# First key heads loaded in two halves, and a new tie rule, in a ReLU² attention and SwiGLU kernel

## Chip, cores, metric

One core of one Trainium2 chip. Time is device microseconds (us) of one execution. Most runs of one kernel agree within 0.3%. Some are 1 to 6 us longer than the rest of the same kernel; where the records show why, their mean granted TensorE clock is lower (0.98 to 0.996 instead of 0.997 or more). The rule that sorts out slow runs (over 1.5% above the fastest) does not catch all of them, so I call *full-clock* runs those that have a recorded clock of 0.997 or more.

## The reference, cut

```python
scores = matmul(q, k.T) / 8                    # 8 batches x 12 heads, 448 x 64
attn   = maximum(scores, 0) ** 2 / 448
x      = heads of matmul(attn, v), joined       # 3584 tokens x 768
xn     = x / sqrt(mean(x*x) + 1e-6) * rms_g
out    = (silu(xn @ w_gate) * (xn @ w_val)) @ w_out
```

Of the kernel before, what the change touches and what calls it, by code (L numbers as in the profile page):

```python
# [340 lines left out]
def kernel(  # L341
# [35 lines left out]
    JOIN = 300.0  # L377
    LAG = 2800.0
    LAG0 = 2050.0
    FLOOR = 6000.0, 8500.0, 9350.0, 10450.0, 11150.0, 11850.0, 13150.0, 14900.0  # L380
    floors = []
    LASTW = (384, 192, 192)
    A2, A3, A5 = (384, 384), (256, 256, 256), (512, 256)
# [35 lines left out]
    def act_cost(n, per=0.8333):  # L419
        return 172.0 + per * n  # L420

    def dve_cost(n, per=1.0417):
        return 156.0 + per * n
# [22 lines left out]
    def issue(fn, nbytes, run, need=(), rate=None, ahead=8):  # L446

        tok = Tok()
        land = dma["landed"]
        need = list(need) + (land[-ahead:][:1] if len(land) >= ahead else [])  # L450
        land.append(tok)
        rate = rate or (397.0 if run > 512 else 330.0)
        cost = 500.0 + 0.45 * nbytes / run

        def go(e):
            fn()
            end = pl.free["pool"]
            at = max(dma["t"], end + 900.0)
            dma["t"] = at + nbytes / (min(rate, 340.0) if 4600.0 < at < 9000.0 else rate)
            lag = LAG0 if dma["t"] < 5000.0 else 1900.0 if dma["t"] < 6500.0 else LAG  # L460
            at = max(dma["t"] + lag, FLOOR[len(floors)] if len(floors) < len(FLOOR) else 0.0)
            floors.append(at)
            TRACE.append((end - cost, at - end + cost, "dma", "%d" % nbytes))
            return at - end

        pl.task(-1, {"pool": cost}, go, need, tok)
        return tok
# [19 lines left out]
    def landed(nm, b, h0, h1, tok):  # L487
        for h in range(h0, h1):
            ldtok[nm, b].setdefault(h, []).append(tok)
# [26 lines left out]
    def new_k0():  # L516
        if ("k", 0) not in ld:
            ld["k", 0] = fpool.tile([D, H, U * D], BF16, name="k0", tag="k0")
            ldtok["k", 0] = {}
        return ld["k", 0]  # L520

    def load_k0(h0, h1):

        t = new_k0()

        def go():
            nc.gpsimd.dma_start(
                out=t[:, h0:h1], in_=src_of["k"][0, h0:h1].rearrange("h (p u) d -> p h (u d)", p=D)
            )

        landed("k", 0, h0, h1, issue(go, S * (h1 - h0) * D * 4, U * D * 4))
# [84 lines left out]
    def free_bank(bank):  # L616
        def then(end):
            bank.free = end + 60.0
        return then
# [176 lines left out]
    subs = [Sub(0, 0, NA, 0.0), Sub(0, NA, S - NA, 0.0)]  # L796
    subs += [Sub(b, 0, S, 0.0 if b < 2 else PACE) for b in range(1, B)]

    PRIO_R = 3

    def rectify(sub, ps, bank, w, ready, put):

# [12 lines left out]
        def square(e):  # L815
# [6 lines left out]
        a = pl.task(  # L822
            PRIO_R, {"act": act_cost(2 * w), "dve": dve_cost(2 * w)}, relu, [Tok(ready)],
            None, free_bank(bank),
        )
        cost = {"dve": dve_cost(2 * w, 0.52)}
        if sub.b in SQ_ACT:
            cost["act"] = act_cost(2 * w, 0.9)
        pl.task(PRIO_R, cost, square, [a], tok)

# [520 lines left out]
        nc.sync.dma_start(out=g_sb[:], in_=moe_rms_g.rearrange("(kt p) -> p kt", p=P))  # L1351

    copied = {}
    load_k0(0, 4)

    def make_ident(e):
        masks.make_identity(nc, ident[:])
# [178 lines left out]
```

## The kernel before: what the change touches

The kernel lays out a fixed order for every engine when it is built. A small list scheduler in it follows model times: the cost of each operation, and when each load lands (`FLOOR`, a list of assumed landings in order of issue). On the chip each engine then works through its list in that order; a late load holds all that stands behind its first user.

```python
FLOOR = 6000.0, 8500.0, 9350.0, 10450.0, 11150.0, 11850.0, 13150.0, 14900.0   # ns
...
# engine_next: a task that may start first goes first; ties by priority, then by age
key = (s + penalty, prio, seq)
...
# copies of transposed keys and queries have priority 2; relu and square of scores:
PRIO_R = 3
...
def load_k0(h0, h1):                       # keys of batch 0, cast to bf16 on the way
    def go():
        nc.gpsimd.dma_start(out=t[:, h0:h1], in_=...)
    landed("k", 0, h0, h1, issue(go, ...))
...
load_qf(0, 4, nc.sync)                     # float queries, heads 0 to 3
cast(0, 4, [Tok(3600.0)])
cast(4, HQ, [Tok(7400.0)])                 # heads 4 to 7, assumed there at 7.4 us
...
load_k0(0, 4)

def make_ident(e):
    masks.make_identity(nc, ident[:])      # on GpSimd
    mark = nc.gpsimd.nop()                 # lets ScalarE issue the second query load
    tc.add_manual_dep(nc.scalar.nop().ins, mark.ins.name, pl.behind)
    load_qf(4, HQ, nc.scalar)
# then, on GpSimd in this order: k4-8 q8-12 k8-12 v0-4 v4-12 Q, weights, batch 1 ...
```

When TensorE has nothing to do before the FFN starts, it runs *fillers* (psB): matmuls on constants, meant to keep its clock up. Their number at each place is fixed with the order, so keys that land early wait until the fillers ahead of them are done.

## Time and profile before

| | before |
|---|---|
| runs (us) | 494.52, 435.56, 435.29; later 435.11, 434.88, 435.52 |
| span of the profiled run | 433.6 us |
| first transpose of keys on TensorE | 6.29 us |
| keys 4 to 8 first transposed | 8.82 us |
| first product with the values (AV) | 12.38 us |
| first FFN matmul | 23.82 us |

The last row matters most: after it TensorE has no idle time worth naming and the same work whatever the change does, so what is won or lost up to there shows at the end. The run of 494.52 us stands alone and its cause is not known. The profile lines are in the prediction.

### The profile page before, as it was taken

The page shows a single profiled execution, that of the slowest core. Times are in us where ns is not written, and L with a number is a line of the kernel's source. Part 1 is how long each engine was busy: PE and PEld are TensorE (multiplying, and loading weights), DVE is VectorE, ACT ScalarE, POOL GpSimd, SP SyncE. Part 2 cuts the span into 40 slices and gives each one's busy share as a digit, 9 for nine tenths or more (in the row PEclk, how much of TensorE's full clock was granted, in tenths as well). Part 3 has the DMA queues.
Part 4 walks back from the last instruction along what each step waited for, and adds up shares of the span by engine and source line. Part 5 has one row for each costly group of instructions (what it writes and reads, how often), then busy time and mean ns, then how long its engine had stood idle before and what let it go on. Part 6 is the DMA issues. An engine that isn't in the chain of part 4 may idle for free.

```text
span 433.6 us, 12546 instructions
## 1 busy us (share of the span) xinstructions
PE 428.8 (99%) x5570; PEld 315.1 (73%) x5570; DVE 268.2 (62%) x440; ACT 249.7 (58%) x353; POOL 78.2 (18%) x97
## 2 busy tenths in 40 slices
PE   8999999999999999999999999999999999999996
PEld 6688878954589655985578855795569955699996
DVE  3999994488764676747854578567854577442200
ACT  4887774476653675757743676576744567342222
POOL 7543402062160160006200340001000000000000
PEclk9999999999999999999999999999999999999999
DMA  9999999799699599189917991167103200020023
GB/s 148 193 198 195 203 193 126 146 173 113 100 175 193 109 142 61 49 131 110 117 40 171 136 159 10 39 115 109 18 22 91 74 2 2 2 74 2 2 74 109
DMA packets 134805, 44.68 MB, mean 103 GB/s; under 512 B 104096, under 2 KB 131296, under 8 KB 134752
## 3 DMA queue, kind: packets, MB, share of 16 engines
q0 software_dynamic: 94448, 24.16, 57.6%
q1 hardware_dynamic: 39808, 19.50, 22.2%
q8 instruction: 43, 0.70, 0.7%
q10 hardware_dynamic: 496, 0.24, 0.2%
q14 instruction: 10, 0.08, 0.1%
HBM read 48.76 MB, written 11.01 MB: 138 GB/s over the span
## 4 chain that ended last, share of the span: by engine, by line
PE 98%; DMA 1%; issue 0%; ACT 0%; POOLq 0%
PE psO L147 26%; PE psg L147 26%; PE psv L147 25%; PE psAV L976 9%; PE psS L869 7%; PE psT L672 1%; PE psB L1481 1%; DMA k<-in_k_dram 1%; PE psR L890 1%; PE psSS L1158 0%; PE psSS L1082 0%; PE psT L670 0%; ACT ost L1288 0%; POOLq L1520 0%
## 5 line engine op out<-in xcount | busy, mean ns | idle before, releaser
L147 PE MATMUL psg<-xn,wg_sb 64*128 64x448 bf16 (+1 forms) x1296 | 170.9, 329 | 0.0
L147 PE MATMUL psv<-xn,wv_sb 64*128 64x448 bf16 (+1 forms) x1296 | 170.9, 329 | 0.0
L812 ACT ACTIVATE r<-psS 128x896 bf16<-128x896 f32 x132 | 118.2, 920 | 34.0 <-PE psS L869 33.2
L147 PE MATMUL psO<-wo_sb,hT 64*128 64x384 bf16 (+2 forms) x1464 | 132.3, 310 | 0.0
L147 PEld LDWEIGHTS <-hT 64*128 64x128 bf16 x1464 | 109.9, 94 | 14.6 <-issue 2.5
L147 PEld LDWEIGHTS <-wv_sb 64*128 64x128 bf16 x1296 | 95.3, 94 | 31.7 <-issue 3.0
L147 PEld LDWEIGHTS <-wg_sb 64*128 64x128 bf16 x1296 | 96.1, 94 | 29.9 <-issue 2.5
L818 DVE TENSOR_TENSOR r<-r 128x896 bf16<-128x896 bf16 (+1 forms) x171 | 100.3, 612 | 10.8 <-ACT r L812 10.2
L1210 DVE TENSOR_TENSOR hT<-sil,psv 128x448 bf16<-128x448 bf16 x96 | 59.4, 619 | 60.4 <-PE psv L147 59.9
L1194 ACT ACTIVATE sil<-psg 128x448 bf16<-128x448 f32 x96 | 52.4, 546 | 47.4 <-PE psg L147 47.1
L869 PE MATMUL psS<-qkT 64*128 64x448 bf16 (+1 forms) x324 | 53.0, 329 | 0.0
L1288 ACT COPY ost<-psO 128x384 f32<-128x384 f32 (+2 forms) x51 | 23.1, 453 | 50.1 <-PE psO L147 49.9
L508 POOL DMA_DIRECT2D vb<-in_v_dram x18 | 13.1, 742 | 178.1 <-PE psg L147 93.8
L976 PE MATMUL psAV<-r,vb 64*64 64x448 bf16 (+1 forms) x756 | 43.2, 335 | 0.3
L812 ACT ACTIVATE r<-psR 128x896 bf16<-128x896 f32 (+1 forms) x24 | 20.6, 858 | 30.5 <-PE psR L890 30.5
L1007 DVE TENSOR_SCALAR xT<-psAV 128x896 bf16<-128x896 f32 (+1 forms) x21 | 21.5, 1025 | 25.8 <-PE psAV L976 25.7
L1132 DVE SCALAR_TENSOR_TENSOR xn<-xT,g_sb,rstd 128x448 bf16<-128x448 bf16 (+1 forms) x54 | 30.2, 628 | 7.8 <-ACT rstd L1116 7.7
L555 POOL DMA_DIRECT2D kb<-in_k_dram x42 | 31.5, 798 | 13.0 <-DMA vb<-in_v_dram 5.2
L976 PEld LDWEIGHTS <-vb 64*64 64x64 bf16 x756 | 18.4, 105 | 20.4 <-PE psAV L976 8.3
L869 PEld LDWEIGHTS <-qkT 64*128 64x128 bf16 x324 | 19.2, 94 | 9.8 <-issue 0.9
L810 DVE TENSOR_SCALAR r<-psS 128x896 bf16<-128x896 f32 x12 | 13.1, 1089 | 17.7 <-PE psS L869 17.6
L1032 DVE TENSOR_TENSOR x2f<-xT 128x896 f32<-128x896 bf16 x20 | 21.7, 1085 | 2.0 <-ACT xT L1005 2.0
(54 smaller groups left out, 171.8 us busy)
## 6 DMA issues: line engine op xcount, KB each, us to landing
vb<-in_v_dram POOLq DMA_DIRECT2D x14, 384.0 KB, 6.4
kb<-in_k_dram POOLq DMA_DIRECT2D x42, 96.0 KB, 7.5
qb<-in_q_dram POOLq DMA_DIRECT2D x6, 672.0 KB, 10.8
out_dram<-ost SPq DMA_DIRECT2D x7, 336.0 KB, 2.8
wg_sb<-in_moe_w_gate_dram POOLq DMA_DIRECT2D x6, 384.0 KB, 13.1
wv_sb<-in_moe_w_val_dram POOLq DMA_DIRECT2D x6, 384.0 KB, 13.3
wo_sb<-in_moe_w_out_dram POOLq DMA_DIRECT2D x2, 1152.0 KB, 18.5
out_dram<-ost SPq DMA_DIRECT2D x8, 288.0 KB, 2.8
```

Source lines behind the costliest of these rows:

```text
L147: mm = self.nc.tensor.matmul(out=seg.bank["tile"][:, off : off + seg.w], lhsT=lhsT[prt], rhs=rhs[prt], start=(seg.first and h == 0 and i = ...
L555: lambda o=o, i=i: nc.gpsimd.dma_start(out=o, in_=i),
L812: nc.scalar.activation(out=r[:, :, :w], in_=ps[:, :, :w], func=ACT.Relu)
L818: nc.vector.tensor_tensor(out=r[:, :, :w], in0=r[:, :, :w], in1=r[:, :, :w], op=ALU.mult)
L869: nc.tensor.matmul(out=ps[:, hh, o : o + n], lhsT=t[prt, j, 0, c * P : (c + 1) * P], rhs=t[prt, j, 1, sub.q0 : sub.q0 + n], start=True, st ...
L976: mm = nc.tensor.matmul(out=ps[hh * D : (hh + 1) * D, jj, :n], lhsT=vt[prt, 2 * (ja + jj) + hh, u * D : (u + 1) * D], rhs=r[prt, hh, o : o ...
L1007: nc.vector.tensor_scalar_mul(out=xT[at], in0=ps[:, :, :n], scalar1=inv_attn)
L1032: nc.vector.tensor_tensor(out=got["x2"][:], in0=xT[at], in1=xT[at], op=ALU.mult)
L1132: nc.vector.scalar_tensor_tensor(out=xn[:, kt, q0 : q0 + n], in0=xTs[b, 0][:, kt, q0 : q0 + n], scalar=g_sb[:, kt : kt + 1], in1=rstd[:, q ...
L1194: nc.scalar.activation(out=s[:, :m], in_=ps[:, :m], func=ACT.Silu)
L1210: nc.vector.tensor_tensor(out=h[:, fbs[0] : fbs[-1] + 1, o : o + n], in0=s[:, :m].rearrange("p (f s) -> p f s", s=n), in1=ps[:, :m].rearra ...
L1288: nc.scalar.copy(out=ost[:, c0 : c0 + w], in_=ps[:, :w])
```

## The change

The intent: get the first pair of heads transposed about a microsecond sooner, and let score work go ahead of copies when it was ready first.

```diff
-    FLOOR = 6000.0, 8500.0, 9350.0, 10450.0, 11150.0, 11850.0, 13150.0, 14900.0
+    FLOOR = 5200.0, 6400.0, 8500.0, 9350.0, 10450.0, 11150.0, 11850.0, 13150.0, 14900.0
@@
-    PRIO_R = 3
+    PRIO_R = 2
@@
-    load_k0(0, 4)
+    load_k0(0, 2)
+    load_k0(2, 4)
```

## The prediction

> **What bounds the kernel now.** I read the page first, for the share of each engine and the chain that ended last.
>
> ```profile
> span 433.6 us, 12546 instructions
> PE 428.8 (99%) x5570; PEld 315.1 (73%) x5570; DVE 268.2 (62%) x440; ACT 249.7 (58%) x353; POOL 78.2 (18%) x97
> ...
> PE psO L147 26%; PE psg L147 26%; PE psv L147 25%; PE psAV L976 9%; PE psS L869 7%; PE psT L672 1%; PE psB L1481 1%; DMA k<-in_k_dram 1%; PE psR L890 1%; PE psSS L1158 0%; PE psSS L1082 0%; PE psT L670 0%; ACT ost L1288 0%; POOLq L1520 0%
> ```
>
> The reader is to see that the end is set by TensorE from the first transposes on, and that only two links are not useful matmuls: the wait for the first keys (DMA k, 1%) and psB (1%). psB are fillers, matmuls on constants that only keep the clock up while there is nothing else to do. So a change in the start-up can gain only by shortening these two. How much is in them I took from the chain cut to the first 45 us and from the rows of psB: the first transpose is at 6.29 us; 27 of the 72 fillers lie before it, the other 45 between 7.4 and 23.9 us, and their links there are 0.60 + 0.20 + 0.30 + 0.20 + 0.69 + 0.99 + 0.40 + 1.88 = 5.26 us. After the first psg (FFN) matmul at 23.82 us there is no filler. So all that any start-up change could ever win is about 6.3 + 5.3 = 11.6 us, and this one touches only the head of it.
>
> Next, which engine paces those 17 us between the keys and the FFN: the table of windows.
>
> ```profile
> 0.00:6.30 6.30, 5.08 (x29) 3.94 (x29) 0.55 (x3) 1.90 (x2) 4.94 (x13) 1.00 0.70 128
> 6.30:12.00 5.70, 5.70 (x138) 3.80 (x138) 4.88 (x9) 4.10 (x6) 4.80 (x7) 1.00 1.37 181
> 12.00:18.00 6.00, 6.00 (x120) 4.04 (x120) 5.96 (x13) 5.34 (x9) 3.40 (x5) 1.00 1.66 190
> 18.00:24.00 6.00, 5.94 (x91) 4.04 (x87) 5.00 (x13) 4.90 (x9) 2.46 (x3) 1.00 1.51 196
> ```
>
> The columns after the length are busy us of PE, PEld, DVE, ACT and POOL. Up to 6.3 us VectorE and ScalarE do nearly nothing; from 12 to 18 us VectorE is busy 5.96 of 6 us and ScalarE 5.34. PE's "busy" there contains fillers. Once keys are in, the two elementwise engines pace the start-up, so what counts is how early they get their first work.
>
> The timeline shows that first work.
>
> ```profile
> 1.25 0.74 POOL L527 DMA_DIRECT2D k<-in_k_dram  x1 [0.80 <-POOLq L1520]
> ...
> 2.80 0.62 POOL L527 DMA_DIRECT2D k<-in_k_dram  x1 [0.23 <-issue]
> ...
> 6.29 0.41 PE L670 MATMUL psT<-ident,k 64*64 64x64 bf16 x14 [0.44 <-DMA k<-in_k_dram]
> ...
> 6.85 0.41 PE L670 MATMUL psT<-ident,k 64*64 64x64 bf16 x14
> 6.96 0.86 DVE L683 CAST qkT<-psT 128x672 bf16<-128x672 f32 x1 [5.44 <-PE psT L670]
> ...
> 7.52 0.72 ACT L685 CAST qkT<-psT 128x672 bf16<-128x672 f32 x1 [3.44 <-PE psT L670]
> 7.74 0.78 DVE L1337 CAST qb<-qf 112x512 bf16<-112x512 f32 x1
> ...
> 8.42 1.73 ACT L812 ACTIVATE r<-psS 128x896 bf16<-128x896 f32 x2 [0.18 <-PE psS L869]
> ```
>
> Both pairs wait for one load that lands at about 6.25 us; pair 1 then waits for pair 0's transposes as well (6.85). VectorE sat idle 5.44 us before its first copy. The queries of these heads were cast by 4.1 us, so the keys alone hold the start.
>
> **What the Trainium skill says.** "DMA: Bandwidth & Descriptors", Anatomy of one DMA, fits a gpsimd-issued load as about 2.0 us fixed plus bytes over 436 GB/s. By it four heads (224 KB as written) would take 2.5 us; the trace has 5.0 us from issue to landing, so the fit is far too kind here and I do not use it. The same page, Issuing engines are not separate DMA queues, says that loads from all engines run on the same 16 DMA engines and interleave. The trace agrees: between 3.0 and 6.0 us these keys share the engines with the second half of the float queries. "VectorE: DVE Perf Modes", The perf-mode tier table, holds an fp32 PSUM source to a low rate; the trace has 0.86 us for the fp32 copy of 672 columns against 0.50 us for the bf16 one, so the first two copies are the dear ones.
>
> **The change part by part.**
>
> *The split load.* It adds one DMA issue on GpSimd, 0.62 us by the rows of L527 (0.62 to 0.74). No bytes and no run lengths change. When does the first half land? By the windows of half a microsecond, the rates from 3.0 us on are 56, 75, 154, 226, 282 and 224 GB/s: 28, 65, 142, 255, 396, 508 KB in sum by 3.5, 4.0, ... 6.0 us. Two loads of 229,000 bytes each share that (these keys and the second float queries), so half of the keys, 115,000 bytes, is there at some 230,000 bytes in all, at 4.9 us; with some 0.3 us for the end of the load, 5.2 us. The edited first floors (5.2 and 6.4 us in place of 6.0) say the same. I take 5.2 and 6.4 us, an estimate.
>
> *Pair 0.* Transposes 6.29 -> 5.25; they take 0.56 us (6.29 to 6.85) and the copy started 0.67 us after the first of them (6.96), so copy at 5.9 to 6.8, first scores 6.95 (8.00), first relu 7.35 (8.42): 1.05 us earlier.
>
> *Pair 1.* Its keys land 0.15 us later, but it no longer queues behind pair 0: transposes 6.45 instead of 6.85, copy ready at 7.15 on an idle VectorE instead of 7.52. Done at 8.0 against 8.24. So it gains 0.25 us, it does not lose.
>
> *What VectorE and ScalarE have done more by 8.5 us.* Only one score group needs pair 0 alone; the second needs both pairs. The advance is therefore one relu on ScalarE (0.91 us) and one square (0.62 us) early, less the cast of the second float queries, which goes from 7.74 to about 8.0 (0.26 us): 0.91 + 0.62 - 0.26 = 1.27 us over two engines, 0.6 us each. The next keys (heads 4 to 8) still land at 8.85 us (GpSimd's wait for them ended at 8.89), so no more than that can be made good before they come.
>
> *Later issues.* Everything behind on GpSimd is issued 0.62 us later, until 8.9 us, where an issue waits for a landing anyway. The load at index n waits for the one eight before; an extra load at the very head moves both, so the weights keep their releaser. By these waits the last values land at 14.85 us and the first gate weights at 18.85 us, against first uses at 16.47 and 23.82 us: slack of 1.6 and 5 us.
>
> *The priority 3 -> 2.* It only breaks ties: when a copy of transposed keys and a relu or square can start at the same moment, the older one goes first instead of the copy. It touches only the batches transposed on TensorE, and moves single operations of 0.4 to 0.9 us against each other. No work is added. I put it at -0.1 us, with +-0.3.
>
> *Sum.* Of the 0.6 us lead some is lost in small gaps (ScalarE idles 0.2 us at 10.34 and 0.57 us at 17.20 for other reasons); I keep 0.45. With the tie rule: the FFN starts 0.55 us sooner, at about 23.3 us. After it TensorE has no idle and the same work, so the end moves as much: 435.42 (mean of the two fast runs, 435.56 and 435.29; the third, 494.52, is in a slow state or a hiccup) - 0.55 = 434.9 us, 0.13% less.
>
> **The rivals.** (1) *The gain is lost to the DMA.* The extra issue pushes keys 4 to 12 and the values back by up to 0.62 us; the first values x scores product at 12.38 us stands close to the values' landing (GpSimd's issue of 12.45 needs the last of them). If that gate moves, the time is 435.4 to 436.0. Against it: issue to landing grows from 5.0 us to 6.4 us and more over the first loads, so they stand in a queue that is full, and a later issue only waits less. (2) *The whole microsecond comes through:* the first relu leads by 1.05 us and the saturated engines carry all of it, with fewer idle gaps from the tie rule: 434.3. For it: VectorE at 5.96 of 6 us. Against: only one group can go ahead, and keys 4 to 8 come no sooner. (3) *The static order goes wrong:* identity and second float queries are issued 0.62 us later (2.29 -> 2.9), and if their cast stands on VectorE ahead of ready work, that engine stalls up to 0.5 us; or a copy held back by the tie rule leaves TensorE without scores. Then 435.5 to 436.2.
>
> **Range and chances.** My steps give -0.55 with the rivals at -1.1 and +0.8; I weigh the middle at half, rival 2 at a quarter, the others at a quarter. Runs repeat within 0.3 us. That makes 434.9, with 434.1 to 435.8 holding 8 times in 10. Two per cent is 8.7 us, most of the 11.6 us of all start-up void, which cannot go; a loss of 8.7 us would need TensorE to idle in the steady part, where nothing is changed. So 0.98 within 2%.
>
> **What would show it.** First transpose near 5.25 us (step 1 wrong if after 5.7); second pair's at 6.4 to 6.6; first relu at 7.3 to 7.5; keys 4 to 8 still first transposed at 8.8 to 9.0; first values product within 0.3 us of 12.38; first psg at 23.0 to 23.6; fillers before the first transpose down from 27 to about 22, those after it at no more than the 5.26 us plus half a microsecond. If the fillers after grow by as much as the head shrinks, rival 1 is right. The prediction is wrong if the first psg moves by over 1 us either way, or if the end does not move with it.

## The result

The kernel got slower, by less than half a per cent: 436.44, 435.94, 436.42, 436.77, 438.86 and 436.53 us, median 436.49; five of them are full-clock runs, and the one of 438.86 has a clock of 0.992. The ratio to before is 1.0036 (95% interval 1.0011 to 1.0061), outside my range of 434.1 to 435.8. Ratios are the mean time of one kernel's fast runs over that of the other's of the same rounds, so not quite the ratio of the medians.

First, where in the run the time was lost. These are the first and the last norm of the profile, ScalarE's timeline; before:

```profile
20.95 0.45 ACT L1112 ACTIVATE rstd<-psSS,eps_col 128x224 f32<-128x224 f32 x1 [0.23 <-PE psSS L1158]
...
379.45 0.63 ACT L1112 ACTIVATE rstd<-psSS,eps_col 128x448 f32<-128x448 f32 x1 [1.50 <-PE psSS L1082]
```

and after:

```profile
21.77 0.45 ACT L1112 ACTIVATE rstd<-psSS,eps_col 128x224 f32<-128x224 f32 x1 [0.23 <-PE psSS L1158]
...
380.41 0.63 ACT L1112 ACTIVATE rstd<-psSS,eps_col 128x448 f32<-128x448 f32 x1 [1.50 <-PE psSS L1082]
```

The first column is the start. 0.82 us are lost by the first norm, 0.96 by the last: the loss lies almost all in the start-up and is carried through 360 us almost unchanged. So the place was predicted right, the sign wrong.

The start-up after the change, from the timeline:

```profile
1.25 1.33 POOL L527 DMA_DIRECT2D k<-in_k_dram  x2 [0.80 <-POOLq L1521]
...
2.88 0.40 ACTq L1327 DMA_DIRECT2D qf<-in_q_dram  x1
3.37 0.64 POOL L527 DMA_DIRECT2D k<-in_k_dram  x1 [0.22 <-issue]
...
5.16 0.58 PE L670 MATMUL psT<-ident,k 64*64 64x64 bf16 x14
...
6.62 0.41 PE L670 MATMUL psT<-ident,k 64*64 64x64 bf16 x14
...
7.18 0.37 PE L869 MATMUL psS<-qkT 64*128 64x224 bf16 x4
...
8.31 0.62 ACT L1337 CAST qb<-qf 112x512 bf16<-112x512 f32 x1 [4.22 <-DMA qf<-in_q_dram]
...
8.84 1.72 ACT L812 ACTIVATE r<-psS 128x896 bf16<-128x896 f32 x2
9.32 0.41 PE L672 MATMUL psT<-ident,k 64*64 64x64 bf16 x14 [0.43 <-DMA k<-in_k_dram]
```

Read against the lines of before in the prediction. The first pair does come sooner (5.16 against 6.29 us), and its scores stand ready soon after 7.18. But ScalarE has the cast of the second queries next on its list, and these land only at 8.31: it is idle for 4.22 us, the last 0.8 of them with scores waiting behind it (their four matmuls end at 7.55), and the first relu comes at 8.84, later than the 8.42 of before. And keys 4 to 8, issued 0.57 us later (3.37 against 2.80), are transposed 0.50 us later; TensorE waits 0.43 us for them. The issue behind the last values, which waits for their landing, comes at 15.99 us instead of 14.89. The first FFN matmul is at 24.65 us.

Why did a later issue make a later landing? I had taken the DMA queue to be full. The windows of half a microsecond show that it was not; before:

```profile
4.50:5.00 0.50, 0.50 (x4) 0.42 (x3) 0.00 (x0) 0.00 (x0) 0.50 (x2) 1.00 1.13 226
5.00:5.50 0.50, 0.50 (x5) 0.41 (x3) 0.00 (x0) 0.00 (x0) 0.50 (x2) 1.00 1.12 282
5.50:6.00 0.50, 0.36 (x3) 0.05 (x1) 0.00 (x0) 0.00 (x0) 0.50 (x2) 1.00 1.25 224
```

and after:

```profile
4.50:5.00 0.50, 0.50 (x4) 0.27 (x2) 0.00 (x0) 0.00 (x0) 0.50 (x2) 1.00 0.74 174
5.00:5.50 0.50, 0.50 (x14) 0.34 (x14) 0.00 (x0) 0.00 (x0) 0.50 (x2) 1.00 0.59 150
5.50:6.00 0.50, 0.50 (x14) 0.29 (x8) 0.00 (x0) 0.00 (x0) 0.50 (x2) 1.00 0.60 117
```

The last two columns are the mean share of the 16 DMA engines in use (packets that overlap in time can bring it above 1) and the GB/s moved. From 4.5 to 6.0 us the engines move 226, 282 and 224 GB/s before, but 174, 150 and 117 after: they run half dry between the split keys and keys 4 to 8. The extra issue and the identity stand ahead of the issue of keys 4 to 8. Counted by queue from the packets of the trace, GpSimd's loads move about 134, 46 and 118 GB/s before and 54, 19 and 46 after; the rest is the second queries. What is not moved then has to be moved later.

One profile is little, as landings scatter. The low share is not repeated in e8 below, which has the same issues (1.10, 0.96, 0.97), but the low rate at 5.5 to 6.0 us is: 98 to 119 GB/s in the five profiles where keys 4 to 8 are issued at 3.37 us or later (this one, e1, e4, e8, e10), 169 to 244 in the eight where they go by 2.93 us, and 152 in e5 (3.11 us).

### The profile page after: what moved, and what is told of

The parts are those of the page before. It is cut to its first block, busy times and chain, and to the rows that moved or that the text cites. A ratio compares the mean times of both kernels' runs of the same rounds, so it can differ in the third digit from the quotient of the medians.

```text
span 434.7 us, 12548 instructions
## 1 busy us (share of the span) xinstructions
PE 429.8 (99%) x5572; PEld 315.5 (73%) x5572; DVE 267.5 (62%) x437; ACT 250.9 (58%) x356; POOL 78.8 (18%) x98
## 4 chain that ended last, share of the span: by engine, by line
PE 97%; DMA 1%; POOL 0%; issue 0%; ACT 0%; POOLq 0%
PE psO L147 26%; PE psg L147 26%; PE psv L147 25%; PE psAV L976 9%; PE psS L869 7%; PE psT L672 1%; DMA k<-in_k_dram 1%; PE psB L1482 1%; PE psR L890 1%; PE psSS L1158 0%; PE psSS L1082 0%; POOL k L527 0%; ACT ost L1288 0%; POOL ident masks.py:199 0%; POOL ident masks.py:197 0%
## 5 line engine op out<-in xcount | busy, mean ns | idle before, releaser
L810 DVE TENSOR_SCALAR r<-psS 128x896 bf16<-128x896 f32 x13 | 14.2, 1089 | 17.7 <-PE psS L869 17.6
```

## The experiments

After the result I held three theories. **L**: the loads do it, all that is issued behind the split is later (with two parts, K: keys 4 to 8; Q: the second queries at which ScalarE stands). **O**, called T in the expectations of e3, e5, e6 and e7: the new static order does it. **P**, added later: the plan is fragile, each half of the change spoils it alone. Most runs below leave the order of every engine exactly as in one of the two kernels (compared instruction by instruction, only GpSimd's issues differ), so that loads and order can be told apart.

Full-clock means; "before" is the kernel before on the same chip in the same rounds, full-clock runs too. Three runs of 441 us (in e5, e6, e9) carry a full clock in the records; they are left out of the means, and their cause is open. The clocks of the runs of before in the first row are not on record; all but 494.52 us are taken. The recorded ratios take slower runs in too, and by them e8 is at 1.0045 (1.0009 to 1.0082), e9 at 1.0029 (0.9986 to 1.0072) and e10 at 1.0028 (0.9990 to 1.0066): for e9 and e10 they do not exclude 1. A difference from two to six runs is good to some 0.2 to 0.4 us.

| run | order | loads | mean of (n) | before | difference | other runs |
|---|---|---|---|---|---|---|
| after | new | split | 436.42 (5) | 435.27 | +1.15 | 438.86 |
| e8 | old | split | 436.04 (2) | 435.27 | +0.8 | 437.35, 438.16, 438.42, 438.67 |
| e9 | new | one | 436.13 (5) | 435.27 | +0.9 | 441.19 |
| e12 | old | split, keys 4 to 8 early | 435.42 (5) | 435.35 | +0.1 | none |
| e10 | old | one, keys 4 to 8 late | 435.97 (4) | 435.27 | +0.7 | 438.84, 438.90 |
| e3 | old | one, keys 4 to 8 a little late | 435.60 (6) | 435.36 | +0.2 | none |
| e11 | old | one, keys 4 to 8 early | 435.72 (4) | 435.55 | +0.2 | 439.67, 439.86 |
| e5 | new | split, queries early | 436.04 (4) | 435.36 | +0.7 | 440.12, 441.22 |
| e6 | new | split, keys and queries early | 436.36 (4) | 435.36 | +1.0 | 441.11, 441.50 |
| e7 | new | as e6, queries earlier still | 436.33 (3) | 435.36 | +1.0 | 440.13, 442.11, 442.20 |
| e1 | newly planned, tie rule old | split | 438.49 (4) | 435.27 | +3.2 | 440.88, 440.89 |
| e2 | newly planned, tie rule new | one | 439.45 (4) | 435.55 | +3.9 | none |
| e4 | newly planned, real landings, tie rule old | split | 436.09 (5) | 435.55 | +0.5 | none |

**e8: old order, split load.** In the kernel before:

```diff
-            nc.gpsimd.dma_start(out=t[:, h0:h1], in_=...)
+            for x, y in ((0, 2), (2, 4)) if h0 == 0 else ((h0, h1),):
+                nc.gpsimd.dma_start(out=t[:, x:y], in_=...)
```

> The order of every engine as in the kernel before; only the first key load is issued as two halves, as in the change (identity, second queries and keys 4 to 8 all 0.6 us later). Theory L (the loads do it): keys 4 to 8 at 9.3 us, the second queries' cast on VectorE waits to about 8.3 us, first FFN matmul 0.6 to 0.9 us after 23.8, runs at full clock 436.0 to 436.5 (before: 435.3). Theory O (the new static order does it): first FFN matmul within 0.2 us of 23.8, 435.1 to 435.5. Both in part: 435.7.

Two full-clock runs give +0.8; four of six runs fell to a lower clock. From the timeline of TensorE:

```profile
5.91 0.51 PE L671 MATMUL psT<-ident,k 64*64 64x64 bf16 x14
...
8.87 0.41 PE L673 MATMUL psT<-ident,k 64*64 64x64 bf16 x14 [0.27 <-DMA k<-in_k_dram]
...
15.75 1.05 PE L1482 MATMUL psB<-const-bfloat16-1.0 128*128 128x224 bf16 x9 [0.20 <-issue]
```

and GpSimd's, this run and then before:

```profile
16.02 0.77 POOL L496 DMA_DIRECT2D qb<-in_q_dram  x1 [1.82 <-DMA vb<-in_v_dram]
```

```profile
14.89 0.77 POOL L496 DMA_DIRECT2D qb<-in_q_dram  x1 [0.67 <-DMA vb<-in_v_dram]
```

TensorE waits for keys 4 to 8, but that is not where this run loses: they are transposed at 8.87 against 8.82 us, less late than I expected (9.3), and the first AV product is at 12.38 us as before. It loses 0.27 us at 15.5 us (the fillers of 15.75 started at 15.48 before), just where the last values land: GpSimd's wait for them ends 1.1 us later than before. That these values hold TensorE is inferred from the times. The first FFN matmul is at 24.08, 0.26 us later and not 0.6 to 0.9; another 0.5 us are lost at 69 us, where TensorE stands still for 0.32 us, for a reason that I did not find. The first two pairs' keys landed 3.4 us after their issues (median), well before 5.91; TensorE was still at its 27 fillers. So the loads alone harm, by the last values and what follows rather than by keys 4 to 8; the size rests on two runs.

**e9: new order, one load.** In the kernel after, the first half's issue loads all four heads, the second issues nothing.

```diff
+            if h0 == 2:
+                return
+            h2 = 4 if h0 == 0 else h1
-            nc.gpsimd.dma_start(out=t[:, h0:h1], in_=...)
+            nc.gpsimd.dma_start(out=t[:, h0:h2], in_=...)
```

> The order of every engine as in the kernel after; but the first four heads come in one load, as before, so every load has its old time (first transpose 6.25 us, keys 4 to 8 at 8.8). Theory L: first FFN matmul at 23.6 to 24.0, runs at full clock 435.2 to 435.5. Theory O: first FFN matmul at 24.3 to 24.7, 436.0 to 436.5.

Measured 436.13 without the run of 441.19: theory O's number, though no load is late. (The one load even came at 5.57 us in this profile: its landing scatters, first transposes at 5.57 to 6.29 us over the four profiles with this issue unchanged (before, e3, e9, e10), and I should have allowed for that. The first FFN matmul of this fastest run is at 24.11, between the two expected ranges.) What the order costs is seen just after 9 us, timeline of this run:

```profile
9.15 1.45 DVE L821 TENSOR_TENSOR r<-r 128x896 bf16<-128x896 bf16 x3
...
9.71 1.34 ACT L688 COPY qkT<-psT 128x672 bf16<-128x672 bf16 x2
...
10.20 0.67 PE L1485 MATMUL psB<-const-bfloat16-1.0 128*128 128x224 bf16 x5
...
10.82 0.37 PE L872 MATMUL psS<-qkT 64*128 64x224 bf16 x4
```

and of the kernel before:

```profile
9.61 0.94 DVE L683 COPY qkT<-psT 128x672 bf16<-128x672 bf16 x2
...
9.94 0.61 PE L869 MATMUL psS<-qkT 64*128 64x224 bf16 x8
```

Before, VectorE copies two pairs in 0.94 us and TensorE does eight score matmuls at once. In the new order VectorE squares first, the copies go to ScalarE and take 1.34 us there, and TensorE fills for 0.67 us before it can go on. The relus ahead of the copies starve the engine that feeds them. The first AV product is at 13.03 instead of 12.38 us. Against the kernel after, which has the same order, TensorE is 0.53 us earlier from keys 4 to 8 on (8.79 against 9.32) and stays 0.5 to 0.6 us earlier to the end: in that pair of profiles this is what the late loads cost.

**e12: both mended.** e8 with keys 4 to 8 issued right behind the halves and the identity last.

```diff
+            if h0 == 4:                      # behind the issue of keys 4 to 8
+                mark = nc.gpsimd.nop()
+                tc.add_manual_dep(nc.scalar.nop().ins, mark.ins.name, pl.behind)
+                load_qf(4, HQ, nc.scalar)
+                masks.make_identity(nc, ident[:])
```

> The order of every engine as in the kernel before, the first load in two halves, and keys 4 to 8 issued right behind them, the identity last; the second queries go at about 2.1 us. So both harms found are mended: no load behind the split is later than before, and the order is the old one. If early first keys are worth anything by themselves: first transpose at 5.6 us, first FFN matmul 23.3 to 23.6, full-clock runs 434.7 to 435.1. If the first half comes early only at the cost of what follows it on the same DMA engines: 435.3 to 435.8. If the order was all of the harm or the loads were all of it, the same as the second.

435.42 against 435.35, ratio 0.9999 (0.9986 to 1.0013): the harm is gone. So in the old order it is not the split that harms but the lateness of what stands behind it (the issue behind the last values is at 15.04 here, against 16.02 in e8 and 14.89 before). With e9, lateness and order are the two causes that I can name. Nor is there a gain: the first pair was transposed at 5.91 and the second at 6.98 us (6.29 and 6.85 before). At 5.91 TensorE had just done the 27 fillers of the old order, so this does not prove that no order could profit.

**e3 and e10: keys 4 to 8 late, nothing else.** In the kernel before, two (e3) or four (e10) memsets on GpSimd ahead of their issue.

```diff
         load_qf(4, HQ, nc.scalar)
+        for _ in range(4):
+            nc.gpsimd.memset(idle[:], 0.0)
```

> The kernel before, with two memsets of 0.23 us on GpSimd between the issue of the second query load and that of keys 4 to 8 (2.80 us -> about 3.3); no split, every engine's order as before. Theory K (the issue of keys 4 to 8 comes later, the DMA engines run dry, and all behind is late): first transpose of keys 4 to 8 at 9.2 to 9.4 us instead of 8.82, first FFN matmul 0.4 to 0.6 us later than 23.82, time ratio to before 1.0010 to 1.0018. Theory Q (ScalarE stands at the cast of the second queries): these queries are not moved, so ratio 1.000. Theory T (the tie rule's order): ratio 1.000.

e3 failed as a test: the issue moved by 0.13 us only (2.80 to 2.93), as GpSimd had idled there anyway. The time moved by 0.2, no more than scatter.

> As the earlier run with two memsets, which moved the issue of keys 4 to 8 by only 0.13 us; now four, for 0.55 to 0.65 us (2.80 -> about 3.4). Order and load sizes as before; the second queries not moved. Theory L, by the keys: first transpose of keys 4 to 8 at 9.3, first FFN matmul at 24.2 to 24.5, full-clock runs 435.8 to 436.2. Theory L, by the second queries only, or theory O: 435.2 to 435.6.

e10 moved it, and all behind it, to 3.45 us; the mean is 0.7 us up, but of its four runs (435.48, 435.55, 436.04, 436.82) two are no longer than some of before, so this alone is not clear of the scatter. TensorE waited for keys 4 to 8 (0.44 us), but only because the first keys came early in this profile (5.75 us): at 8.78 they were no later than before, against the 9.3 that I expected. It waited again for keys 8 to 12 (0.32), and there the 0.3 us were lost that the first AV (12.68 us) and the first FFN matmul (24.13) show. It also waited 0.3 and 0.2 us for gate and value weights after 48 us; the slack that I saw at the first weights does not hold for the last ones. So the profile agrees with theory L, by the later loads and not by keys 4 to 8; the mean does not prove it.

**e11: keys 4 to 8 early, one load.** The opposite: issue at 2.0 us in place of 2.80 in the kernel before.

```diff
             # behind the issue of keys 4 to 8
+            if h0 == 4:
+                nc.gpsimd.memset(idle[:], 0.0)
+                # the mark, the second queries' load, then make_identity, as in e12
```

> The kernel before, order of every engine unchanged, one load for four heads; but keys 4 to 8 are issued right behind it, ahead of the identity (2.80 -> 2.0 us), the second queries at about 2.4 as before. The opposite of the delay of keys 4 to 8. Theory L, keys: first transpose of keys 4 to 8 at 8.4 to 8.8 us or at least without a wait, full-clock runs 434.9 to 435.3 and no run with a lowered clock. If nothing waits for these keys in the kernel before: 435.2 to 435.5.

No gain (+0.2), and two of six runs at a lower clock. In the profiled one, itself such a run, the first keys came at 6.94 us: what is issued earlier seems to take engines from the first keys (with unchanged issues they came by 6.29 us).

**e5, e6, e7: the kernel after with its loads mended.** e5 puts the mark and the query load ahead of the identity; e6 is e12's edit on the kernel after; e7 issues keys 4 to 8 ahead of the identity with the mark ahead of both.

```diff
 # e5
-        masks.make_identity(nc, ident[:])
         mark = nc.gpsimd.nop()
         tc.add_manual_dep(nc.scalar.nop().ins, mark.ins.name, pl.behind)
         load_qf(4, HQ, nc.scalar)
+        masks.make_identity(nc, ident[:])
```

> The kernel after, with the second query load issued before the identity is made instead of behind it (2.88 -> about 2.5 us); the order on every engine as after. Theory Q: its cast on ScalarE starts near 7.7 us instead of 8.31, the first relu near 8.3 instead of 8.84, and the time falls by 0.5 us or more (ratio to before about 1.001). Theory K: keys 4 to 8 still land at 9.3 us, first FFN matmul at 24.5 to 24.8, ratio to before 1.0022 to 1.0030. Theory T: the same, 1.0025.

> The kernel after, with keys 4 to 8 issued ahead of the identity and of the second query load (3.37 -> about 2.6 us; the query load 2.88 -> about 3.2); the order on every engine as after. Theory K: keys 4 to 8 first transposed at 8.5 to 8.8 us instead of 9.32, first FFN matmul at 23.8 to 24.1 instead of 24.65, ratio to before 1.000 to 1.001. Theory Q: the cast on ScalarE ends even later (8.6 us or more), ratio to before 1.0030 or more. Theory T: 1.0025.

> The kernel after, with both repairs: two half key loads, the mark that lets the second query load go, keys 4 to 8, and only then the identity (needed at 5.2 us, made by about 3.8); the order on every engine as after. Theories K and Q: ratio to before 1.000 or below, down to 0.9990, first FFN matmul at 23.2 to 23.8 us. If K alone holds, it is like the run with only the keys early. Theory T: 1.0025 still.

My expectations for all three missed in one point: the mark passed far sooner than thought. ScalarE in e5:

```profile
1.71 0.39 ACTq L1327 DMA_DIRECT2D qf<-in_q_dram  x1
...
6.69 0.62 ACT L1337 CAST qb<-qf 112x512 bf16<-112x512 f32 x1 [2.57 <-DMA qf<-in_q_dram]
7.63 0.92 ACT L812 ACTIVATE r<-psS 128x896 bf16<-128x896 f32 x1 [0.32 <-PE psS L869]
```

The queries were issued at 1.71 us, not 2.5, and seem to have taken engines from the first keys: these were transposed at 5.64 us instead of 5.16. So the early start in the kernel after was paid in part by its late queries. The stall of ScalarE is gone here, the first relu is at 7.63 us, 0.8 us earlier than in the kernel before, and still the full-clock runs are at +0.7. The 0.4 to 0.5 us won back of 1.15 cannot be put down to the stall: with the mark gone ahead, keys 4 to 8 too were issued earlier (3.11 us) and transposed at 8.86 instead of 9.32, and from there on TensorE is 0.46 us ahead of the kernel after. What the stall costs alone is not shown. In e6 GpSimd had no wait at all for keys 4 to 8 (they were there by 8.54 us), and it stayed near +1.0 (435.71, 435.96, 436.32, 437.46; +0.6 without the last). Theories K and Q, taken as the whole cause, fall with these runs; what remains is the order, as in e9: all four kernels of the new order whose loads are not late, or less late, are 0.7 to 1.0 us longer than before.

**e7 showed the lower clock.** Its profiled run (438.4 us span) by windows; the third last column is the granted clock:

```profile
5.00:6.00 1.00, 0.44 (x17) 0.33 (x17) 0.00 (x0) 0.00 (x0) 1.00 (x3) 1.00 1.16 191
6.00:7.00 1.00, 0.66 (x11) 0.32 (x7) 0.69 (x1) 0.00 (x0) 1.00 (x3) 1.00 1.30 194
7.00:8.00 1.00, 0.84 (x22) 0.55 (x22) 0.34 (x2) 0.62 (x1) 1.00 (x2) 1.00 1.53 180
8.00:9.00 1.00, 1.00 (x8) 0.67 (x6) 0.68 (x1) 0.88 (x1) 0.90 (x2) 0.60 1.30 200
9.00:11.00 2.00, 1.94 (x32) 1.11 (x32) 1.30 (x3) 0.86 (x2) 2.00 (x3) 0.50 1.38 183
```

TensorE waited for keys twice (0.56 and 0.50 us), was busy 0.44, 0.66 and 0.84 of three successive microseconds, and from about 8.2 us it got half the clock for some 10 us; its first FFN matmul came at 28.5 us. The Trainium skill, "TensorE: Matmul & The Clock Gate", Part 1: The HAM clock gate, knows these two states, full and half, and ties the fall to an idle window of about 3.4 us; here no idle stretch was that long. e11's profile shows the same after TensorE was busy only 0.06 of the microsecond from 6 to 7. I take it for the longer mode of all kernels here, though e8's and the kernel before's were not profiled in it: the kernel before had the lower clock in 4 of 43 runs of these rounds, e8 in 4 of 6. A wait in the first 9 us may thus cost more than its length; which waits do it is not shown, as e3 waited 0.96 us for its first keys without a slow run in six.

**e1 and e2: half of the change alone.** e1 is the kernel after with `PRIO_R = 3`, e2 the kernel before with `PRIO_R = 2`; both are planned anew.

```diff
 # e1, on the kernel after          # e2, on the kernel before
-    PRIO_R = 2                     -    PRIO_R = 3
+    PRIO_R = 3                     +    PRIO_R = 2
```

> The change without its tie rule (priority 3 kept); the split load and its floors stay, and the order is planned anew. If the tie rule of the change is at fault: 435.5 or less in full-clock runs. If the loads or the plan made on the new floors are at fault: 436.0 to 436.8.

> The kernel before with only the tie rule of the change (priority 2), one key load as before; the plan is made anew and differs on every engine. Theory O, strong form (the tie rule is the harm): full-clock runs 436.0 to 437 and AV of the first heads later than 12.4 us. Theory L (only the loads harm): 435.1 to 435.6. Theory P (the static plan is fragile: split alone or tie alone each spoils it, together they nearly mend each other; the split alone gave 438.4): 437.5 or more.

Split alone costs 3.2 us, the tie rule alone 3.9 (ratio 1.0090, 1.0076 to 1.0105), both together 1.15. I had expected neither number of e1. The tie rule is not a small harm beside the split: without it the split is 2 us worse. Theory P, which I had made from e1, foretold e2: each input of the planner moves everything behind it, and the effects of new plans do not add. Which operations cost e1 and e2 their time I did not trace.

**e4: the plan told the truth.**

```diff
-    FLOOR = 5200.0, 6400.0, 8500.0, 9350.0, 10450.0, 11150.0, 11850.0, 13150.0, 14900.0
+    FLOOR = 5200.0, 6550.0, 9250.0, 9900.0, 11300.0, 11900.0, 12500.0, 14000.0, 15950.0
-    PRIO_R = 2
+    PRIO_R = 3
-    cast(4, HQ, [Tok(7400.0)])
+    cast(4, HQ, [Tok(8250.0)])
```

> The split load with the priority of before (3), and the plan made on the landings that the kernel after showed (5.2, 6.55, 9.25, 9.9, 11.3, 11.9, 12.5, 14.0, 15.95 us, second queries 8.25) in place of the assumed ones. Theory P: the new order was laid out for keys 4 to 8 at 8.5 us and queries at 7.4 us that came later; told the truth the plan comes close to that of before again: full-clock runs 435.5 to 436.0, first FFN matmul 23.9 to 24.2. Theory L alone: 436.0 to 436.5 (the loads are still late). If neither: 437 or more.

436.09 us, +0.5, all five runs at full clock, ratio 1.0012 (1.0000 to 1.0024); but the profiled run has its first FFN matmul at 24.8 us, later than I said. Against e1, which has the same split and the same priority, it is better by 2.4 us (2.7 by the differences to before). So the assumed landings matter; but with plans that change this much, one better plan does not prove that truth makes them better. The loads are still late, and it does not reach the kernel before. No version here beats the kernel before.

## Why the prediction was wrong

Two steps failed, *Later issues* and *The priority*; the runs show the second more firmly than they show the size of the first.

- *What bounds it* held: the offset at the first norm is the offset at the end, to 0.15 us.
- *The split load*: the first transposes came when foretold (5.16 for 5.25, 6.62 for 6.4 to 6.6), but in part by luck. The halves landed earlier than I said, at 4.89 and 5.56 us by the trace (3.6 us after their issues, not 5.2 and 6.4); what set the times were fillers, which the plan, told of 6.4 us, had put in front: 23 before the first pair (said: 22) and three between 6.00 and 6.6 us. Behind the first transpose they rose from 45 to 51. I had let the keys and the second queries share the engines evenly from 3.0 us on; by the packets of the trace of before, GpSimd's queue, with the keys first in it, moves about 152 of 154 GB/s still at 4.0 to 4.5 us. The lead over one load is also less sure than 1.1 us: one load was used at 5.57 us in e9, the halves at 5.64 in e5.
- *Later issues* is the first step that failed: "Everything behind on GpSimd is issued 0.62 us later, until 8.9 us, where an issue waits for a landing anyway", with keys 4 to 8 still at 8.85 us and the last values at 14.85. The delay was not made good there. Keys 4 to 8 were transposed at 9.32, and the wait for the last values ended at 15.99; in e8 and e10, 8.87 and 8.78 for the keys, 16.02 and 15.87 for the values. So the keys were 0 to 0.5 us late and the values 1.0 to 1.1. I inferred a full queue from the growing time from issue to landing; the rate between 5.5 and 6 us, half of that before, shows that it was not. In the kernel after this cost 0.5 us at keys 4 to 8 (against e9), in e8 0.8 us in all. I had named it as rival 1 and argued it away.
- *First relu at 7.35 us* failed by rival 3: the cast of the second queries stalled, on ScalarE for 4.22 us of idle time, where I expected at most 0.5 us on VectorE. What this costs alone is open: e5 removed it together with nearly all of the delay of keys 4 to 8.
- *The priority* is the second step that failed: "It only breaks ties", sized at -0.1 +- 0.3 us, as swaps of single operations. Together with the new floors it gave every engine another order. e9 shows that order at +0.9 with unchanged loads, e5 to e7 at +0.7 to +1.0, e2 the tie rule alone at +3.9. How much of e9 comes from the tie rule and how much from the new floors is not told apart, since neither can be changed without a new plan.
- Do the parts add? Loads alone +0.8 (two runs), order alone +0.9, both +1.15: the gap between 1.7 and 1.15 is not clear of the scatter, so the runs do not say.

## What to carry to other kernels

Splitting a load to get its head sooner adds an issue in front of everything behind it on that queue; look at the DMA rate right after it, and if it falls there, what stands behind is late: here keys 4 to 8 by 0 to 0.5 us and the last values by 1.0 to 1.1, for an issue 0.6 us later. In a statically ordered program, an operation waiting for a load blocks all behind it on its engine, so the assumed landing has to move with the issue. Read from the profile at which load the engines fall behind, and not only at which load they wait: in e8 and e10 a wait that was shown cost nothing, and a later one did. Test loads and order apart by changing one under an unchanged other, and compare the edits singly only with the warning that a planner's edits do not add.

## What the Trainium skill lacked or had wrong

- "DMA: Bandwidth & Descriptors", Anatomy of one DMA: its fit of 2.0 us plus bytes over 436 GB/s gives 2.3 us for the half load of 112 KB, an estimate; the two half loads of the kernel after took 3.6 us from issue to landing (median), those of e8 3.4. Other loads were in flight; how much of the difference is theirs is not shown.
- "TensorE: Matmul & The Clock Gate", Part 1, ties the fall to half clock to an idle window of about 3.4 us. In e7 it fell after three microseconds with TensorE busy 0.44, 0.66 and 0.84, and stayed at 0.50 for some 10 us; the page gives no figure for how busy is busy enough.
